# Half-size products for the keys of five more batches, with streamed weight sums and a new order inside a batch

## The chip, the core and the metric

One Trainium2 chip, one of its cores. The time is the device time of one launch, in microseconds (us). Five engines work side by side, each through its own list of instructions in order: TensorE (PE in the profile, with its weight loads as PEld), VectorE (DVE), ScalarE (ACT), GpSimd (POOL) and SyncE (SP), which issues the DMAs here. They wait for each other through semaphores.

## What is computed

Per batch (8 of them, 8 heads of width 64, 512 local and 32 global positions): windowed attention with global tokens, and behind it a feed-forward block on the joined heads (`d_model` 512, `d_ff` 1024).

```python
k_all = np.concatenate([k_g, k_l], axis=2); v_all = np.concatenate([v_g, v_l], axis=2)
out_g = sm(scale * q_g @ k_all.T) @ v_all
s_ll = np.where(np.abs(pos[:, None] - pos[None, :]) <= 32, scale * q_l @ k_l.T, -1e9)
out_l = sm(np.concatenate([scale * q_l @ k_g.T, s_ll], axis=-1)) @ np.concatenate([v_g, v_l], axis=2)
...
x_prev = x shifted by one position
xk = mu_k * x + (1.0 - mu_k) * x_prev
xr = mu_r * x + (1.0 - mu_r) * x_prev
k = np.maximum(xk @ w_k, 0.0)
v = k * k @ w_v
r = 1.0 / (1.0 + np.exp(-(xr @ w_r)))
return r * v
```

## The kernel before

The feed-forward block works on columns of 256 tokens (`TOK`), two halves per batch, and at the end on the 256 global tokens of all batches together. Each float32 operand is held as two float32r parts, a high one (`h`, a cast on ACT) and a low one (`l`, the difference, a subtraction on POOL or DVE, `split`), and a product is three matmuls: high by high, high by low, low by high. A matmul here is 128x128 weights by 128x256 tokens.

For a half batch, `mix` (L509) makes `xk` and `xr`: on DVE one difference and two scaled sums per 256 columns (L518, L522), an ACT cast (L526) and a POOL subtraction (L527). `squares` (L551) multiplies by the weights `w_k`, which stay in SBUF: 4 groups of 48 = 2x8x3 matmuls into a PSUM bank, then relu on ACT (L560) and a square on POOL (L561). `gates` (L564) takes 48 matmuls, with a copy on DVE (L577) and a sigmoid on ACT.

From batch `FROM` = 2 on, the values (the product with `w_v`) of the two halves of a batch are done together by Strassen's scheme: the 2x2 blocks of the weights (A11 to A22, and the sums S1 to S4, computed once) times the blocks of the squared keys (B11 to B22, and differences T1 to T4). Seven products of 24 matmuls stand for eight. The weight blocks lie in DRAM (`scratch`) and are loaded for each product in two parts of 512 KB into a ring of five buffers (`load_left`, L264). The token blocks are split by `Keys.split` (L635): B blocks on DVE, T blocks on POOL. `values_1` (three products) runs ahead of the keys of the first half of the next batch, `values_2` (four) ahead of those of the second, and their results are gathered by ACT copies and DVE additions (L670 to L698).

The heads of batch b+1 run beside the feed-forward of batch b: `together` advances the two streams by their share of steps. Scores land in PSUM, DVE masks them (L329), ACT takes exponentials (L335), POOL normalises (L344), PE transposes them into one bank (`ps_t`), from which ACT and DVE copy in turn (L383), and PE weights the values. The order on each engine's list is fixed when the program is built, by a list scheduler that follows the order of the code, its priorities and its own durations. SP issues all DMAs in one such list; a DMA that waits holds up those behind it. The last batch has no heads beside it, and the global tokens come last (`end`, L966).

Of the kernel before, what the change touches and what calls it, by code (L numbers as in the profile page):

```python
# [9 lines left out]
F32 = mybir.dt.float32  # L10
# [4 lines left out]
I64 = mybir.dt.int64  # L15
# [40 lines left out]
def local_global_attention_then_rwkv_ffn(  # L56
# [34 lines left out]
    ps2 = ctx.enter_context(tc.tile_pool(name="ps2", bufs=2, space=PSUM))  # L91
# [6 lines left out]
    FIRST_USE = {"m": [ps2] * 2, "s": [ps4] * 4, "t": [ps1, psx], "o": "t"}  # L98
    MIDDLE_USE = {"m": [ps2, ps2, psx], "s": [ps4] * 4, "t": [ps1], "o": "s"}
    LAST_USE = {"m": [ps2, ps2, psx, ps4, ps4, ps4, ps4]}  # L100
# [47 lines left out]
    wk_h = const.tile([P, NC, DF], F32R, name="wk_h")  # L148
    wk_l = const.tile([P, NC, DF], F32R, name="wk_l")

    early_w, early_u = ExitStack(), ExitStack()
    first_chunks = early_w.enter_context(tc.tile_pool(name="first_chunks", bufs=1, reuse_waits="tile"))
# [13 lines left out]
    def load_chunk():  # L168
        n = load_chunk.n
        if n < len(chunks):  # L170
            if n < EARLY:
                w64 = first_chunks.tile([P, CH], I64, tag=f"w64_{n}", name="w64")
            else:
                w64 = stage.tile([P, CH], I64, tag="w64", name="w64")
            nc.sync.dma_start(out=w64, in_=chunks[n][0])
            staged.append(w64)
            load_chunk.n += 1
# [41 lines left out]

    FROM = 2  # L220
    LEFT = ("A11", "A21", "A12", "A22", "S2", "S3", "S4", "S1")
    HC = NF // 2
    scratch = dramp.tile([P, len(LEFT), HC, 2, TOK], F32, name="scratch")

    def behind(store):
        tc.add_manual_dep(
            store.ins, Tokens.square.ins.name,
            mybir.DependencyInfo(mybir.DependencyClass.Sync, mybir.DependencyReason.DATA),
        )

    def sums_of_values():

        for i in range(HC):
            a = stage.tile([P, 2, 2, TOK], F32, tag="w64", name="a")
            hs, ls = (stage.tile([P, 4, TOK], F32R, tag="w64", name=f"{x}s") for x in "hl")
            for j in range(2):
                f = i + j * HC
                for x, part in enumerate((wv_h, wv_l)):
                    part = part[:, f].bitcast(F32).rearrange("p (e n) -> p e n", e=2)
                    store = nc.sync.dma_start(out=scratch[:, 2 * j:2 * j + 2, i, x], in_=part)  # L240
                    behind(store)
                with tc.issue_after(Tokens.square.ins):
                    nc.gpsimd.tensor_add(  # L243
                        a[:, j], *(w[:, f].bitcast(F32).rearrange("p (e n) -> p e n", e=2) for w in (wv_h, wv_l))
                    )
            a11, a21, a12, a22 = (a[:, j, e] for j in range(2) for e in range(2))

            nc.gpsimd.tensor_add(a22, a21, a22)
            nc.gpsimd.tensor_sub(a21, a11, a21)
            nc.gpsimd.tensor_sub(a11, a22, a11)  # L250
            nc.gpsimd.tensor_sub(a12, a12, a11)
            s = a.rearrange("p j e n -> p (j e) n")
            nc.scalar.copy(hs, s)
            nc.vector.tensor_sub(ls, s, hs.bitcast(F32))
            for x, part in enumerate((hs, ls)):
                nc.sync.dma_start(out=scratch[:, 4:8, i, x], in_=part.bitcast(F32))
            yield

    V1 = (("A11", "B11"), ("A12", "B21"), ("S2", "T2"))
    V2 = (("S3", "T3"), ("S1", "T1"), ("A22", "T4"), ("S4", "B22"))  # L260
    to_load = [a for a, _ in V1 + V2] * (B - FROM) + ["A11", "A21", "A12", "A22"]
    left = []

    def load_left():  # L264
        if to_load:
            a = LEFT.index(to_load.pop(0))
            for i in range(0, HC, 2):
                part = leftp.tile([P, 2, 2, TOK], F32R, tag="a", name="a")
                nc.sync.dma_start(out=part.bitcast(F32), in_=scratch[:, a, i:i + 2])
                left.append(part)  # L270
# [226 lines left out]
    class Tokens:  # L497
# [5 lines left out]
        def two(self, pool, name, dtype=F32, tag="tmp"):  # L503
            return pool.tile([P, 2, TOK], dtype, tag=tag, name=name)
# [4 lines left out]
        def mix(self):  # L509

            got = []
            for mu, nm in ((mu_k_sb, "k"), (mu_r_sb, "r")):
                got.append((mu, self.wide(f"x{nm}h", F32R), self.wide(f"x{nm}l", F32R)))
            for c0 in range(0, NC, 2):
# [4 lines left out]
                for mu, hi, lo in got:  # L519
                    xf = self.two(tmpp, "xfull")  # L520
                    for j in range(2):
# [3 lines left out]
                        )  # L525
                    nc.scalar.copy(hi[:, both], xf)  # L526
# [74 lines left out]

    class Keys:


        def __init__(self, tokens):
            self.tokens = tokens
            self.k, self.parts = {}, {}

# [5 lines left out]
        def block(self, name):  # L614
            if name in ("B12", "B22"):
                tag = {"B12": "kkh0", "B22": "kkh2"}[name]
                self.k[name] = [self.tokens[0].two(mlp, name, tag=tag) for _ in range(2)]
# [5 lines left out]
        def keys(self, t):  # L623
# [11 lines left out]
        def split(self, *names):  # L635
            for b in names:
                self.parts[b] = []
                for val in self.k[b]:
                    tags = Keys.PARTS[Keys.n_parts % len(Keys.PARTS)]
                    Keys.n_parts += 1  # L640
                    h, l = (self.tokens[0].two(mlp, f"b{x}", F32R, tag) for x, tag in zip("hl", tags))
# [3 lines left out]
        def product(self, out, b, fresh=True):  # L645
            right = self.parts.pop(b)
            for i in range(HC):
                a, (b_h, b_l) = left[i // 2], right[i // 2]
                for j in range(2):
                    a_h, a_l = (a[:, i % 2, x, j * P:(j + 1) * P] for x in range(2))  # L650
                    for n, (w, x) in enumerate(((a_h, b_h), (a_h, b_l), (a_l, b_h))):
                        nc.tensor.matmul(  # L652
                            out[:, j], w, x[:, i % 2], start=fresh and (i, j, n) == (0, 0, 0),
                            stop=(i, n) == (HC - 1, 2), skip_group_check=True,
                        )
            del left[:HC // 2]
            load_left()

        def bank(self):
            return psum("m").rearrange("p (j n) -> p j n", j=2)  # L660

        def sum(self):
            return sump.tile([P, 2, TOK], F32, tag="sum", name="sum")

        def values_1(self):
            t = self.tokens[0]
            X, Y = self.bank(), self.bank()
            self.product(X, "B11")
            c11, self.u2 = self.sum(), self.sum()
            nc.scalar.copy(c11, X)  # L670
            yield
            self.product(Y, "B21")
            nc.vector.tensor_add(c11, Y, c11)
            t.write(0, c11)
            yield
            self.product(X, "T2", fresh=False)
            nc.scalar.copy(self.u2, X)
            yield
            self.split("T3", "T1", "T4")

        def values_2(self):
            t0, t1 = self.tokens
            u2, u3 = self.u2, self.sum()
            X, Y = self.bank(), self.bank()
            self.product(X, "T3")
            nc.vector.tensor_add(X, X, u2)
            nc.scalar.copy(u3, X)
            self.split("B22")
            yield
            self.product(Y, "T1")  # L690
# [345 lines left out]
```

## Time and profile before

| | us |
|---|---|
| three runs: median (lowest, highest) | 715.65 (714.83, 717.27) |
| the profiled execution, whole | 714.27 |
| its span, first to last instruction | 712.1 |
| PE busy in the span | 670.7 |
| DVE, ACT, POOL busy | 413.5, 421.4, 412.8 |

A busy PE in this profile is not PE at its peak: matmuls overlap, and each lasts about 280 ns in the rows although the next starts much sooner. So PE's cost is read from starts, not from busy time. DVE and POOL rows can hold waiting too: an instruction that was issued and could not go on counts as busy. A stage of a batch with heads beside it shows twice, as two halves of some 38 us.

### The profile page before, as it was taken

What the parts mean: (1) busy time and instruction counts of PE and PEld (TensorE: products, weight loads), DVE (VectorE), ACT (ScalarE), POOL (GpSimd) and SP (SyncE); (2) the same over time, 40 slices, a digit from 0 to 9 for tenths busy, and PEclk for the clock granted to TensorE, in tenths of its full rate; (3) what the DMA queues carried; (4) which work ended last, traced back from release to release, by engine and by line L of the source; (5) the groups of instructions that cost most, each with busy time, mean ns of one, the idle gap of its engine ahead of it and who ended that gap; (6) DMA issues with size and microseconds to landing.
All of it is one profiled execution on the core that took longest, in us unless ns stands there. A gap on an engine that the chain in (4) does not pass through costs nothing.

```text
span 712.1 us, 18675 instructions
## 1 busy us (share of the span) xinstructions
PE 670.7 (94%) x7472; PEld 627.4 (88%) x7472; DVE 413.5 (58%) x1180; ACT 421.4 (59%) x1135; POOL 412.8 (58%) x415
## 2 busy tenths in 40 slices
PE   5779899999899899889999999999999999999997
PEld 3568788889798899789999999999989999999896
DVE  5757886346647563756566365735674556276441
ACT  5857787547556557664848384767567553442530
POOL 6556595236858555565567655585558444854730
PEclk9669999999999999999999999999999999999999
DMA  8731635052756652270928265554827090535666
GB/s 344 278 118 37 246 97 216 31 187 83 234 175 201 220 194 75 85 271 8 356 83 282 76 257 188 170 186 143 304 92 265 2 332 24 192 119 164 197 195 200
DMA packets 43542, 123.37 MB, mean 173 GB/s; under 512 B 4032, under 2 KB 20928, under 8 KB 43456
## 3 DMA queue, kind: packets, MB, share of 16 engines
q1 hardware_dynamic: 43456, 122.18, 49.1%
q8 instruction: 59, 0.97, 0.6%
q14 instruction: 27, 0.22, 0.1%
HBM read 104.86 MB, written 17.30 MB: 172 GB/s over the span
## 4 chain that ended last, share of the span: by engine, by line
PE 46%; ACT 16%; DVE 14%; POOL 10%; issue 7%; DMA 6%; POOLq 0%; SPq 0%; ACTq 0%; DVEq 0%
PE ps_m L652 13%; PE ps_m L495 7%; PE ps_m L493 7%; PE ps_m L494 7%; PE ps_s L360 7%; ACT Pt L335 6%; DVE xfull L522 5%; POOL B L561 2%; DVE diff L518 2%; PE ps_t L381 2%; DMA a<-scratch 2%; POOL Pt L344 1%; DMA w<-w_r 1%; DVE B L633 1%; POOL a L243 1%
## 5 line engine op out<-in xcount | busy, mean ns | idle before, releaser
L493 PE MATMUL ps_m<-xkh,wk_h 128*128 128x256 f32 x544 | 154.4, 285 | 5.3 <-ACT gate L573 1.9
L495 PE MATMUL ps_m<-xkh,wk_l 128*128 128x256 f32 x544 | 152.7, 281 | 0.0
L494 PE MATMUL ps_m<-xkl,wk_h 128*128 128x256 f32 x544 | 152.2, 280 | 0.4 <-POOL xkl L527 0.4
L652 PE MATMUL ps_m<-bh,a 128*128 128x256 f32 x736 | 136.3, 281 | 1.5 <-DMA a<-scratch 0.9
L335 ACT ACTIVATE Pt<-Pt,m 128x160 f32<-128x160 f32 x256 | 106.4, 418 | 21.5 <-DVE m L329 21.4
L652 PEld LDWEIGHTS ps_m<-bh,a 128*128 128x128 f32 x736 | 114.3, 188 | 3.7 <-issue 1.5
L344 POOL TENSOR_TENSOR Pt<-Pt,ssum 128x512 f32<-128x512 f32 x64 | 68.2, 1065 | 82.7 <-DVE ssum L293 80.0
L493 PEld LDWEIGHTS ps_m<-xkh,wk_h 128*128 128x128 f32 x544 | 102.9, 190 | 7.8 <-ACT gate L573 2.3
L494 PEld LDWEIGHTS ps_m<-xkl,wk_h 128*128 128x128 f32 x544 | 103.0, 189 | 0.7 <-POOL xkl L527 0.7
L495 PEld LDWEIGHTS ps_m<-xkh,wk_l 128*128 128x128 f32 x544 | 103.1, 189 | 0.0
L652 PE MATMUL ps_m<-bl,a 128*128 128x256 f32 x368 | 102.8, 279 | 0.0
L561 POOL TENSOR_TENSOR B<-relu 128x512 f32<-128x512 f32 x52 | 56.3, 1089 | 39.1 <-ACT relu L560 39.0
L493 PE MATMUL ps_m<-xrh,wr_h 128*128 128x256 f32 x272 | 78.3, 288 | 0.0
L495 PE MATMUL ps_m<-xrh,wr_l 128*128 128x256 f32 x272 | 77.8, 287 | 0.0
L494 PE MATMUL ps_m<-xrl,wr_h 128*128 128x256 f32 x272 | 77.3, 284 | 0.0
L527 POOL TENSOR_TENSOR xkl<-xfull,xkh 128x512 fp32r<-128x512 f32 x34 | 45.3, 1333 | 54.1 <-ACT xkh L526 38.1
L560 ACT ACTIVATE relu<-ps_m 128x512 f32<-128x512 f32 x52 | 31.0, 596 | 76.7 <-PE ps_m L495 73.9
L329 DVE CUSTOM_DVE_ANT_0 Pt<-ps_s,masks 128x160 f32<-128x160 f32 x256 | 65.5, 317 | 8.9 <-PE ps_s L360 8.7
L652 PEld LDWEIGHTS ps_m<-bl,a 128*128 128x128 f32 x368 | 69.1, 188 | 0.6 <-issue 0.6
L518 DVE TENSOR_TENSOR diff<-xT 128x256 f32<-128x256 f32 x64 | 41.9, 693 | 33.7 <-ACT xT L485 19.9
L203 ACT CAST bh<-B 128x512 fp32r<-128x512 f32 x76 | 45.4, 625 | 16.2 <-PE ps_m L652 13.7
L495 PEld LDWEIGHTS ps_m<-xrh,wr_l 128*128 128x128 f32 x272 | 51.8, 191 | 3.0 <-issue 2.8
(144 smaller groups left out, 1639.2 us busy)
## 6 DMA issues: line engine op xcount, KB each, us to landing
a<-scratch SPq DMA_DIRECT2D x92, 512.0 KB, 6.0
raw_qk<-qk SPq DMA_DIRECT2D x32, 768.0 KB, 5.7
raw_v<-v SPq DMA_DIRECT2D x32, 640.0 KB, 5.9
out_l<-gate SPq DMA_DIRECT2D x32, 256.0 KB, 4.9
w<-w_k SPq DMA_DIRECT2D x8, 512.0 KB, 9.8
w<-w_v SPq DMA_DIRECT2D x8, 512.0 KB, 5.2
w<-w_r SPq DMA_DIRECT2D x4, 512.0 KB, 4.9
scratch<-wv_h SPq DMA_DIRECT2D x8, 256.0 KB, 2.9
```

Of the source, the lines that this page charges most:

```text
L203: nc.scalar.copy(hi, val)
L329: read = nc.vector.tensor_tensor_reduce(out=Pt[:, i], in0=place(e, t, h), in1=masks[:, e, slots[t][1]], op0=ALU.add, op1=ALU.min, scale=-s ...
L335: nc.scalar.activation(Pt[:, i], Pt[:, i], AF.Exp, bias=low_x[:, i:i + 1], scale=-1.0, accum_out=ssum[:, i:i + 1],)
L344: nc.gpsimd.tensor_mul(out, Pt[:, each, at:at + n], rinv.unsqueeze(2).to_broadcast([P, 4, n]))
L360: self.last = nc.tensor.matmul(*a, **kw)
L493: nc.tensor.matmul(out, w_h[:, i, cols], x_h(i), start=(i == 0), stop=False)
L494: nc.tensor.matmul(out, w_h[:, i, cols], x_l(i), start=False, stop=False)
L495: nc.tensor.matmul(out, w_l[:, i, cols], x_h(i), start=False, stop=(i == n - 1))
L518: nc.vector.tensor_sub(self.shape(diff[:, j]), self.cur(c0 + j), self.prev(c0 + j))
L527: nc.gpsimd.tensor_sub(lo[:, both], xf, hi[:, both].bitcast(F32))
L561: nc.gpsimd.tensor_mul(k2[f0 // HC][f0 % HC // 2], rk, rk)
L652: nc.tensor.matmul(out[:, j], w, x[:, i % 2], start=fresh and (i, j, n) == (0, 0, 0), stop=(i, n) == (HC - 1, 2), skip_group_check=True,)
```

## The change

From batch 3 on (`FROM` + 1) the keys too are done by seven products instead of eight. The weight blocks of `w_k` and their sums are made during batch 2 (`sums_of_keys`) into a second DRAM tensor, and `w_k` leaves SBUF after that. All weight blocks, 14 parts for the values and 14 for the keys of a batch, come through one ring of six buffers of 512 KB. The token side of the keys is mixed as four blocks for the whole batch, subtracted on DVE and split on ACT and POOL (`mixed`, `x_split`). Both kinds of product go through `seven`, on three PSUM banks. A batch now goes: values of the batch before, gate of half 0, keys, gate of half 1. The last keys of the global tokens are plain products with loaded blocks.

```diff
-    FIRST_USE = {"m": [ps2] * 2, "s": [ps4] * 4, "t": [ps1, psx], "o": "t"}
-    MIDDLE_USE = {"m": [ps2, ps2, psx], "s": [ps4] * 4, "t": [ps1], "o": "s"}
+    FIRST_USE = {"m": [psa, psb], "s": [ps4] * 4, "t": [ps1, psx], "o": "t"}
+    MIDDLE_USE = {"m": [psa, psb, psx], "s": [ps4] * 4, "t": [ps1], "o": "s"}
...
+    def sums(home, tag, parts, out, first, after):
+        a = home.tile([P, 2, 2, TOK], F32, tag=tag, name="a")
...
+            add = first.tensor_add(a[:, j], parts(0, j), parts(1, j))
...
+        nc.gpsimd.tensor_add(a22, a21, a22)
+        nc.gpsimd.tensor_sub(a21, a11, a21)
+        nc.gpsimd.tensor_sub(a11, a22, a11)
+        nc.gpsimd.tensor_sub(a12, a12, a11)
...
+    for b in range(FROM, B - 1):
+        plan(of_values, [a for a, _ in SEVEN])
+        plan(of_keys, [a for a, _ in SEVEN], True)
...
+    def product(out, right, fresh=True):
+        for i, (b_h, b_l) in enumerate(right):
+            a, home = left.pop(0)
...
+            load_left(home)
+            yield
+    def seven(right, done):
+        X, Y, Z = new_bank(), new_bank(), new_bank()
...
+        yield from product(X, right("B11"))
+        copy(c11, X)
+        yield from product(Y, right("B21"))
+        add(Y, c11, 0, 0)
+        yield from product(X, right("T2"), fresh=False)
+        copy(u2, X)
+        yield from product(Z, right("T1"))
+        copy(w, Z)
+        yield from product(X, right("T3"), fresh=False)
+        add(X, w, 1, 1)
+        yield from product(Z, right("B22"), fresh=False)
+        add(Z, u2, 0, 1)
+        yield from product(X, right("T4"), fresh=False)
+        done(1, 0, X)
...
+        def mixed(self):
+            B11, B21, B12, B22 = (self.xv[f"B{i}{j}"] for j in (1, 2) for i in (1, 2))
+            self.x_split("B11", B11)
+            self.x_split("B21", B21)
+            nc.vector.tensor_sub(B11, B12, B11)
+            nc.vector.tensor_sub(B12, B22, B12)
+            self.x_split("B22", B22)
+            nc.vector.tensor_sub(B22, B22, B11)
+            self.x_split("T2", B22)
+            self.x_split("T1", B11)
+            nc.vector.tensor_sub(B21, B21, B22)
+            self.x_split("T3", B12)
+            self.x_split("T4", B21)
+        def x_split(self, name, val):
+            self.x[name] = h, l = [Tokens.two(kxp, f"x{name}{x}", F32R, name + x) for x in "hl"]
+            split(val, h, l, nc.gpsimd)
...
+                def done(i, j, v):
+                    if in_psum(v):
...
+                    else:
+                        nc.vector.scalar_tensor_tensor(blocks[i, j][n], v, 0.0, v, op0=ALU.max, op1=ALU.mult)
...
-        for n, t in enumerate(this.tokens):
-            t.mix()
-            if b > FROM:
-                yield from (before.values_1, before.values_2)[n]()
...
-            yield from this.keys(t)
...
+        this.mix(0)
+        for n, _ in enumerate(before.values()):
+            yield
+            if n == 4:
+                this.mix(1)
+            if n == 8:
+                this.mixed()
+        yield from this.tokens[0].gates()
...
+        yield from this.keys()
+        this.split("B11", "B21")
+        this.differences()
+        this.split("T2")
+        yield from this.tokens[1].gates()
```

How the lists of the engines change. The first place is POOL's list where the keys of a batch end and the values of it begin. Before (batch 5; `B` is a block of squared keys, `xkl` and `xrl` low parts of the mixed tokens, `bl` low part of a value operand, `Pt` the attention weights):

```order
L561 TENSOR_TENSOR B_7321<-relu 128x512
L204 TENSOR_TENSOR bl<-T_7528,bh 128x512
L561 TENSOR_TENSOR B_7322<-relu 128x512
L527 TENSOR_TENSOR xkl<-xfull,xkh 128x512
L344 TENSOR_TENSOR Pt<-Pt,ssum 128x4x128
L344 TENSOR_TENSOR Pgl<-Pt,ssum 128x128
L344 TENSOR_TENSOR Pt<-Pt,ssum 128x4x128
L344 TENSOR_TENSOR Pgl<-Pt,ssum 128x128
L527 TENSOR_TENSOR xrl<-xfull,xrh 128x512
L418 TENSOR_SCALAR Pg<-Pg,ssumg 128x576
```

The same place in the change, from the square of the last product of the keys on (`xB11l`, `xT1l` and the like are low parts of the keys' token blocks):

```order
L742 TENSOR_TENSOR B_7280<-relu 128x512
L205 TENSOR_TENSOR xB11l<-xB_7843,xB11h 128x512
L571 TENSOR_TENSOR xrl<-xfull,xrh 128x512
L205 TENSOR_TENSOR xB21l<-xB_7844,xB21h 128x512
L571 TENSOR_TENSOR xrl<-xfull,xrh 128x512
L205 TENSOR_TENSOR bl<-T_7759,bh 128x512
L571 TENSOR_TENSOR xrl<-xfull,xrh 128x512
L205 TENSOR_TENSOR bl<-B_7279,bh 128x512
L205 TENSOR_TENSOR xT1l<-xB_7843,xT1h 128x512
L205 TENSOR_TENSOR bl<-B_7279,bh 128x512
L205 TENSOR_TENSOR xB22l<-xB_8039,xB22h 128x512
L205 TENSOR_TENSOR bl<-B_7281,bh 128x512
```

The splits of the whole next batch now stand between those of the values, up to T4's (`bl<-B_7280`, eleven rows further on); before, a half batch's mix stood here and the other half's came half a batch later.

The second place is DVE's list at the same time, behind the last addition of the keys, up to a part of what stands ahead of the next copy of transposed weights (`PT<-ps_t`):

```order
L744 SCALAR_TENSOR_TENSOR B_7282<-u_7471 128x512
L771 TENSOR_TENSOR B_7279<-B_7282,B_7279 128x512
L560 TENSOR_TENSOR diff<-xT 128x256 x2
L771 TENSOR_TENSOR T_7759<-B_7284,B_7279 128x512
L771 TENSOR_TENSOR B_7282<-B_7284,B_7282 128x512
L564 SCALAR_TENSOR_TENSOR xB_7843<-diff,mu_k_sb,xT 128x256
L564 SCALAR_TENSOR_TENSOR xfull<-diff,mu_r_sb,xT 128x256
L564 SCALAR_TENSOR_TENSOR xB_7843<-diff,mu_k_sb,xT 128x256
L564 SCALAR_TENSOR_TENSOR xfull<-diff,mu_r_sb,xT 128x256
L205 TENSOR_TENSOR bl<-B_7280,bh 128x512
L518 COPY xg_all<-ps_s 128x2x32
```

Both halves' mixes, 24 instructions, now follow here in one run; before, each half's twelve stood apart.

The third place is PE's list in batch 5 of the change, with the semaphores it waits for, early in the values' last product (T4). The L531 to L533 rows are matmuls of the gate, L469 transposes the global attention weights:

```order
L532 MATMUL ps_m<-xrl,wr_h 128x256
L533 MATMUL ps_m<-xrh,wr_l 128x256
L531 MATMUL ps_m<-xrh,wr_h 128x256
L469 MATMUL ps_t<-ident,Pg 128x128 [waits Activation_49]
L469 MATMUL ps_t<-ident,Pg 128x128 x3
L654 MATMUL ps_m<-bl,a 128x256 [waits Pool_49]
L654 MATMUL ps_m<-bh,a 128x256 x2
```

The product's first matmul stands ahead of ten matmuls of the gate, of which three are shown; its second one waits for POOL's split of T4. Before, keys stood between a split on POOL and the product that used it.

334 lines of the change are left out of this document (185 added, 149 removed).

## The prediction

> **What bounds the kernel now.** I read the page's totals first, then a table by stage, then single rows of the timeline. The page:
>
> ```profile
> span 712.1 us, 18675 instructions
> PE 670.7 (94%) x7472; PEld 627.4 (88%) x7472; DVE 413.5 (58%) x1180; ACT 421.4 (59%) x1135; POOL 412.8 (58%) x415
> L493 PE MATMUL ps_m<-xkh,wk_h 128*128 128x256 f32 x544 | 154.4, 285 | 5.3 <-ACT gate L573 1.9
> a<-scratch SPq DMA_DIRECT2D x92, 512.0 KB, 6.0
> ```
>
> PE is busy almost all the time and nothing else is near it. The table by stage (columns: length, then busy time of PE, PEld, DVE, ACT, POOL with counts, granted clock, DMA share, GB/s) says where it isn't:
>
> ```profile
> 240.00:280.00 40.00, 40.00 (x469) 38.23 (x468) 20.65 (x77) 27.65 (x83) 16.93 (x18) 1.00 0.43 151
> 280.00:318.40 38.40, 33.38 (x405) 30.91 (x404) 24.11 (x69) 23.50 (x65) 26.65 (x25) 1.00 0.46 163
> 438.00:476.30 38.30, 38.05 (x452) 36.05 (x451) 22.07 (x70) 24.89 (x69) 26.44 (x26) 1.00 0.50 166
> 476.30:514.50 38.20, 38.15 (x454) 36.63 (x453) 22.20 (x70) 24.36 (x68) 20.37 (x21) 1.00 0.58 208
> 650.00:665.00 15.00, 13.74 (x117) 13.36 (x115) 14.16 (x20) 4.02 (x7) 8.27 (x6) 1.00 0.32 95
> ```
>
> In the steady batches (third and fourth row, the halves of one) PE idles 0.3 us in 76.5. It idles 5.0 us where the values first go by half-size products (second row) and 1.3 us early in the end stage (last row). So PE bounds the steady batches, and matmuls taken away are worth their spacing. The chain that ended last gives that spacing:
>
> ```profile
> 636.64 5.44 PE ps_m L652 x48
> 601.43 4.02 PE ps_s L360 x117
> ```
>
> 48 matmuls in 5.44 us are 0.1133 us each, and not the 285 ns that one lasts. The 456 matmuls of a batch take 51.7 us; the rest of the 76.5, 24.8 us, is two pairs of heads, 12.4 each. The second row is the largest piece of a pair, the weighting.
>
> **Matmuls taken away.** The keys of a half batch are 96 matmuls (L493 to L495: 544 of each is 17 halves of 32). A batch's 192 become two times seven products of 12, 168. Five batches (3 to 7) save 120, and 120 x 0.1133 is **-13.6 us**. The products of global keys keep their 96.
>
> **The port that DVE and POOL share.** The work around the matmuls decides what is left of this. Here is a place of before where DVE, POOL and PE meet:
>
> ```profile
> 284.99 1.51 DVE L633 TENSOR_TENSOR B<-B,B 128x512 f32<-128x512 f32 x1 [3.64 <-POOL B L561]
> 286.43 1.52 DVE L633 TENSOR_TENSOR T<-B,B 128x512 f32<-128x512 f32 x1
> 288.48 0.68 DVE L383 COPY PT<-ps_t 128x512 f32<-128x512 f32 x1
> ...
> 283.92 3.48 POOL L561 TENSOR_TENSOR B<-relu 128x512 f32<-128x512 f32 x3
> ...
> 289.21 0.44 PE L390 MATMUL ps_t<-ident,Pgl 128*128 128x128 f32 x2 [1.93 <-DVE PT L383]
> ```
>
> While POOL's three squares run (283.92 to 287.40), two DVE subtractions take 1.5 us each; the copy behind them is late, and PE waits 1.93 us for it. Alone, such work starts faster. DVE first, then POOL:
>
> ```profile
> 650.84 0.69 DVE L633 TENSOR_TENSOR T<-B,B 128x512 f32<-128x512 f32 x1 [2.09 <-POOL B L561]
> 651.45 0.69 DVE L633 TENSOR_TENSOR B<-B,B 128x512 f32<-128x512 f32 x1
> ...
> 458.23 0.76 DVE L518 TENSOR_TENSOR diff<-xT 128x256 f32<-128x256 f32 x2 [2.54 <-ACT xT L485]
> 458.91 0.48 DVE L522 SCALAR_TENSOR_TENSOR xfull<-diff,mu_k_sb,xT 128x256 f32<-128x256 f32 x1
> 459.31 0.48 DVE L522 SCALAR_TENSOR_TENSOR xfull<-diff,mu_r_sb,xT 128x256 f32<-128x256 f32 x1
> ...
> 667.24 1.30 POOL L527 TENSOR_TENSOR xkl<-xfull,xkh 128x512 fp32r<-128x512 f32 x1
> 668.49 1.29 POOL L527 TENSOR_TENSOR xrl<-xfull,xrh 128x512 fp32r<-128x512 f32 x1
> ...
> 676.02 2.04 POOL L561 TENSOR_TENSOR B<-relu 128x512 f32<-128x512 f32 x2
> ...
> 298.55 0.40 POOL L344 TENSOR_TENSOR Pgl<-Pt,ssum 128x128 f32<-128x128 f32 x1
> 298.90 1.04 POOL L344 TENSOR_TENSOR Pt<-Pt,ssum 128x512 f32<-128x512 f32 x1
> ...
> 303.85 0.74 POOL L418 TENSOR_SCALAR Pg<-Pg,ssumg 128x576 f32<-128x576 f32 x1 [1.04 <-DVE ssumg L293]
> ```
>
> From start to start: a 512-column DVE operation with both operands in SBUF 0.60, a difference 0.34, a scaled sum 0.40; a POOL split 1.25, a square 1.02, `Pt` with `Pgl` 1.35, `Pg` 0.74. A DVE operation that reads PSUM runs beside POOL's at its normal time:
>
> ```profile
> 463.98 0.68 DVE L383 COPY PT<-ps_t 128x512 f32<-128x512 f32 x1
> ...
> 464.00 1.27 POOL L204 TENSOR_TENSOR bl<-B,bh 128x512 fp32r<-128x512 f32 x1
> ```
>
> So I count POOL's work and DVE's two-SBUF work as one queue. How exact that is: three squares alone are 3.06 us and took 3.48 with one DVE subtraction slipped between, so that 0.60 cost 0.42.
>
> **What the new order puts into one stretch.** Take a steady batch of the change (4, 5, 6), from the last matmul of the keys to the second half of the values' last product, T4, which waits for POOL. Before its split POOL's list holds 7 splits of key blocks, 4 of `xr`, 7 of value parts and a gate product (19 x 1.25 = 23.8), a square (1.0), two `Pt` pairs (2.7) and one `Pg` (0.7): 28.2 us. DVE's list holds, up to the addition which the same product waits for, 8 differences (2.7), 16 scaled sums (6.4) and 12 operations of 512 columns (7.2): 16.3. The queue is **44.5 us**. It starts about 0.9 us before the last keys' matmul, at the addition behind the sixth product. PE has 196 matmuls there (22.2) and one pair of heads (12.4): 34.6. The wait is 44.5 - 0.9 - 34.6 = **9.0 us** a batch if nothing overlaps. With DVE's part at 0.42 for 0.60 it is 11.4 instead of 16.3, and the wait 4.1. Neither row is nearer, and I take the middle, 6.5. Queued behind the waiting matmul are the rest of the gate, the weighting of heads and the next keys, all of PE's work, so nothing covers it. Before, the same work was spread over both halves, with a mix of 12 DVE operations each, and fitted.
>
> [...]
>
> Batch 3 has less on POOL (23.0) and 16.4 on DVE against 198 matmuls (22.4) and most of a pair (11.6): 0 to 4.5 us, middle 2.3. In batch 7, without heads, POOL has 24.6 and DVE 19.0 against 257 matmuls (29.1) and one weighting (4.0): 3.9 to 9.6, middle 6.8. New waits: 2.3 + 3 x 6.5 + 6.8 = **28.6 us** (16.2 to 41.1).
>
> **Waits that go.** The 5.0 and 1.3 us of the table by stage lie in stretches counted anew: **-6.3 us**.
>
> **The rest.** The sums of the keys' weights in batch 2 add 16 small POOL operations, 8 additions of 512 columns and 4 of 1024 on DVE, some 23 us of the queue, in a stage (240 to 280) where PE never idles and POOL is busy 16.9 of 40. If all of DVE's 20.65 there were two-SBUF work, 60.6 would have to fit in 40, 20.6 over; with half of it, 10 over, of which the batch's later half takes some. I take 0, since its results are due only in batch 3, and keep 6 for the range. ACT has 19 operations of some 0.6 us more in five batches, and with 24.9 busy of 38.3 room for them beside PE. Between two products on bank X stands one of 12 matmuls (1.36 us), in which ACT must copy 512 columns:
>
> ```profile
> L670 ACT COPY sum<-ps_m x6: 562/578/586, 303.5 to 664.8; 128x512 f32<-128x512 f32 x6
> ```
>
> Its 0.58 us fit, with 0.8 to spare; 0 is taken, and what it costs if ACT is late is a rival. SP issues 78 more loads of weight parts and 24 stores.
>
> Sum, against the profiled execution's 714.27 (712.1 span and 2.2 around it; the median of the runs is 1.4 higher): -13.6 + 28.6 - 6.3 = +8.7, **723 us**. By the ends of the waits, -3.7 to +21.2: 710.6 to 735.5.
>
> **The rivals.**
> *The queue doesn't reach PE* (other side). Gate matmuls hoisted into gaps and DVE work done earlier could hide it: the place is the same stretch, and it decides where the waits sum to less than the 19.9 us that the matmuls and the waits gone are worth, four a batch. For it: in before, the steady halves hold POOL 26.4 and DVE 22.1 in 38.3, and PE doesn't idle. Against it: the lists, in which T4's split comes behind all key splits. With 6 us left of the new waits: 714.3 - 19.9 + 6 = 700.
>
> *Loads bound PE.* 170 parts instead of 92, 14 per kind of product with one every 1.36 us, and a part lands 6.0 us after issue. Six buffers give five parts ahead, 6.8 us. Before, with five, PE waited in its last run of products:
>
> ```profile
> 702.72 0.35 PE L652 MATMUL ps_m<-bh,a 128*128 128x256 f32 x1 [0.45 <-DMA a<-scratch]
> 300.00:310.00 10.00, 8.58 (x157) 8.18 (x157) 2.32 (x9) 7.25 (x17) 6.42 (x7) 1.00 0.85 319
> ```
>
> At 319 GB/s for a share of 0.85, a pair of `qk` loads (1.5 MB) holds the queues 4.2 us, which leaves 3.4 us of wait after 0.8 of margin. Half of the sixteen pairs of loads in batches 3 to 6 falling on products cost 27: 714.3 - 13.6 + 27 = 728, if the shared port costs nothing. Against it: heads between the products stretch the lead.
>
> *Three banks turn too slowly.* If ACT's copy comes 1.1 us late, 0.3 over the margin, at four turns of each of ten key products of seven, that is 12 us, and the gain is gone: 713.
>
> **How the numbers follow.** Queue 0.58 (723, 711 to 736), hidden queue 0.25 (700), loads 0.09 (728), banks 0.08 (713). About 0.3%, 2.1 us, is what a measurement of this kernel can tell from no change. Of the first case I give 0.50 to slower, 0.05 to same, 0.03 to faster, as its low end lies below no change; with the loads 0.09 to slower and 0.01 of the banks: slower 0.60. Faster is 0.25 and 0.03, 0.28; same 0.12. The range goes from 700, which cuts half of the hidden queue, to 738, the upper end with part of batch 2's 6 us. The likeliest case's own range is 711 to 736.
>
> **What would show it.** Right: PE idles for POOL's `bl` or a DVE copy or addition around the values' last products, 4 to 9 us in each of batches 4 to 7; DVE's differences and scaled sums there last over 1 us. Wrong: steady batches of about 73.8 us with PE idle under 1 us (the first rival); idle time ended by DMA `a` (the second), or by ACT copies of `u2` and `w` in the keys (the third). The saving is right if the steady batch, less its waits, is 2.7 us shorter than 76.5.

## The result and the profile after

The changed kernel takes **760.29 us** (median of 4 runs, 759.36 to 763.87) and the kernel before, on the same chip, 715.63 (4 runs, 714.83 to 717.27): 1.063 times the time, 95% interval 1.0591 to 1.0669. It is slower, as forecast, but by 45 us and not by 9. The profiled executions differ as much: 759.94 against 714.27.

The page of the changed kernel, its totals, two of its groups (busy us, mean ns of one, idle time before and what ended it) and its loads of weight parts (KB each, us from issue to landing):

```profile
span 757.8 us, 18783 instructions
PE 679.9 (90%) x7352; PEld 632.1 (83%) x7352; DVE 517.3 (68%) x1266; ACT 434.3 (57%) x1154; POOL 439.9 (58%) x416
L560 DVE TENSOR_TENSOR diff<-xT 128x256 f32<-128x256 f32 x64 | 52.6, 859 | 9.3 <-ACT xT L523 9.2
L564 DVE SCALAR_TENSOR_TENSOR xfull<-diff,mu_r_sb,xT 128x256 f32<-128x256 f32 x64 | 49.8, 798 | 2.1 <-POOL xkl L571 2.1
a<-scratch_v SPq DMA_DIRECT2D x92, 512.0 KB, 5.2
a<-scratch_k SPq DMA_DIRECT2D x78, 512.0 KB, 4.7
```

PE does 120 matmuls fewer and is busy 9 us longer; DVE is busy 104 us longer with only 86 instructions more. The loads land sooner, in 5.2 and 4.7 us against the 6.0 of before, although there are 78 more.

The table by stage (length, then busy time of PE, PEld, DVE, ACT, POOL with counts, granted clock, DMA share, GB/s). First the kernel before, from 240 us to its end:

```profile
240.00:712.10 472.10, 459.06 (x5107) 441.32 (x5105) 259.26 (x705) 265.21 (x689) 265.61 (x247) 1.00 0.50 171
```

Then the changed kernel: the same stage, its parts between the ends of pairs of heads (batch 2's keys and gates with the first of batch 3's values, then batches 3 to 6 with their overlaps, then batch 7 and the end), and last a stretch of the values and one of the keys:

```profile
240.00:757.80 517.80, 466.95 (x4999) 444.58 (x4997) 362.54 (x796) 274.65 (x706) 292.62 (x250) 0.96 0.73 249
231.50:322.30 90.80, 80.23 (x896) 74.67 (x894) 63.09 (x151) 53.24 (x140) 64.55 (x63) 0.96 0.69 239
322.30:399.60 77.30, 71.67 (x827) 66.24 (x820) 57.50 (x153) 46.92 (x136) 41.65 (x38) 0.98 0.75 251
399.60:477.90 78.30, 72.49 (x842) 68.46 (x841) 58.54 (x152) 47.29 (x137) 45.42 (x40) 0.96 0.80 267
477.90:564.50 86.60, 77.45 (x884) 73.30 (x882) 63.54 (x155) 50.93 (x142) 49.06 (x43) 0.94 0.77 256
564.50:646.70 82.20, 71.62 (x794) 68.64 (x793) 58.55 (x112) 41.62 (x101) 42.50 (x35) 0.96 0.72 233
646.70:757.80 111.10, 99.26 (x844) 98.65 (x843) 67.76 (x87) 37.67 (x64) 56.03 (x40) 0.97 0.71 255
...
480.00:500.00 20.00, 11.53 (x98) 10.76 (x98) 20.00 (x41) 11.66 (x21) 14.32 (x11) 0.77 0.39 115
520.00:540.00 20.00, 20.00 (x276) 19.32 (x275) 8.69 (x30) 11.82 (x32) 0.06 (x1) 1.00 0.90 301
```

All of the 45.7 us lie after 240 us (517.8 - 472.1). PE's idle time there went from 472.1 - 459.1 = 13.0 to 517.8 - 467.0 = 50.9, **+37.8**. Its busy time rose by 7.9 although the stage holds 108 matmuls fewer (5107 - 4999, 12.2 us; at 240 us the changed kernel is 12 matmuls behind, 1.4 us). So **20.1** us of busy time are new as well. The last two rows show where: at 480 to 500, in the values, where the lists of DVE and POOL are both full (the crowded stretch, or the crowd, from here on), DVE is busy without a break and PE for 11.5 of 20; at 520 to 540, in the keys, PE is full, DVE half idle and POOL has nothing to do.

The waits of PE in the changed kernel after 240 us (us in total, times, longest):

```profile
PE ps_t L428 <- DVE PT L421: 24.0, 7, 6.7
PE ps_m L654 <- ACT u L679: 8.0, 1, 8.0
PE ps_t L419 <- ACT PT L421: 7.7, 4, 3.1
PE ps_s L400 <- DVE xT L520: 2.6, 1, 2.6
...
PE ps_m L654 <- DMA a<-scratch_k: 0.9, 1, 0.9
```

The largest is the turn of the one bank of the transposes: `Pgl` can't be transposed into it until DVE has copied `PT` out. One such wait in the timeline, PE, then DVE and POOL:

```profile
407.48 0.28 PE L654 MATMUL ps_m<-bl,a 128*128 128x256 f32 x1
413.29 0.69 PE L428 MATMUL ps_t<-ident,Pgl 128*128 128x128 f32 x2 [5.54 <-DVE PT L421]
...
414.42 0.63 PE L654 MATMUL ps_m<-bh,a 128*128 128x256 f32 x2
414.85 0.41 PE L654 MATMUL ps_m<-bl,a 128*128 128x256 f32 x1
415.06 0.63 PE L654 MATMUL ps_m<-bh,a 128*128 128x256 f32 x2
...
405.79 2.36 DVE L564 SCALAR_TENSOR_TENSOR xfull<-diff,mu_r_sb,xT 128x256 f32<-128x256 f32 x2
408.07 1.75 DVE L720 TENSOR_TENSOR xB<-xB,xB 128x512 f32<-128x512 f32 x1
409.75 2.89 DVE L560 TENSOR_TENSOR diff<-xT 128x256 f32<-128x256 f32 x2
412.56 0.68 DVE L421 COPY PT<-ps_t 128x512 f32<-128x512 f32 x1
...
407.83 1.45 POOL L571 TENSOR_TENSOR xrl<-xfull,xrh 128x512 fp32r<-128x512 f32 x1
409.24 1.72 POOL L643 TENSOR_TENSOR gate<-c,gate 128x512 f32<-128x512 f32 x1
410.91 1.44 POOL L571 TENSOR_TENSOR xrl<-xfull,xrh 128x512 fp32r<-128x512 f32 x1
```

Two things are to be read here. The `PT` copy itself takes 0.68 as ever (all 32 of them on DVE last 676 to 693 ns), but stands behind five DVE operations with both operands in SBUF, 2.1 us of work at their times alone (two of 0.40, one of 0.60, two of 0.34) by the prediction's rows. Here they take 6.8 us, about as long each as one of POOL's operations beside them, which last 1.44 to 1.72. And when PE goes on, three matmuls take 0.64 us (414.42 to 415.06), 0.213 each instead of 0.1133: **half clock**. The granted clock over this and the next such stretch:

```profile
412.00:419.00 7.00, 5.71 (x46) 5.37 (x50) 5.98 (x24) 5.79 (x22) 3.22 (x4) 0.51 0.74 192
490.00:501.00 11.00, 6.02 (x29) 6.03 (x30) 10.96 (x27) 5.67 (x16) 8.99 (x7) 0.53 0.23 73
```

There are seven stretches of half clock after 240 us (from 275, 302, 343, 412, 490, 579 and 664 on), 3.4 to 10.2 us long, one at each of the seven waits of 2.55 us or more that end there: five of them set in before the wait's end, those from 275 and 343 on 0.3 and 1.0 us after it. Before had none there: its clock is 1.00 in the first row of the stage table. The seven are 40.8 us long together, and PE is busy for 29.6 of them at a granted clock of 0.50, so they cost about 15 us of the 20.1. The other 5 are slightly wider spacing elsewhere, which I can't assign. The length of a wait alone doesn't decide: a wait of 2.72 us that ends at 239.4 us in the same profile, and one of 2.03 at 236 us in the kernel before, were followed by a clock of 1.00.

Three of the seven stretches (from 275, 302 and 343 on) are 3.4 us long, three (from 412, 579 and 664 on) 6.8 and the one from 490 on 10.2. The shortest wait that one came with is 2.55 us here, and 1.8 in run e10.

The wait of 8.0 us in batch 7 comes by way of ACT, whose copy `u` frees a bank of the products:

```profile
663.76 2.88 DVE L564 SCALAR_TENSOR_TENSOR xfull<-diff,mu_r_sb,xT 128x256 f32<-128x256 f32 x2
...
666.68 0.62 ACT L570 CAST xrh<-xfull 128x512 fp32r<-128x512 f32 x1 [2.19 <-DVE xfull L564]
667.20 0.58 ACT L679 COPY u<-ps_m 128x512 f32<-128x512 f32 x1
```

The copy stands behind a cast that waits for DVE's late `xfull`.

### The profile page after: what moved, and what is told of

The parts are those of the page before. It is cut to its first block, busy times and chain, and to the rows that moved or that the text cites. A ratio compares the mean times of both kernels' runs of the same rounds, so it can differ in the third digit from the quotient of the medians.

```text
span 757.8 us, 18783 instructions
## 1 busy us (share of the span) xinstructions
PE 679.9 (90%) x7352; PEld 632.1 (83%) x7352; DVE 517.3 (68%) x1266; ACT 434.3 (57%) x1154; POOL 439.9 (58%) x416
## 4 chain that ended last, share of the span: by engine, by line
PE 46%; DVE 26%; ACT 14%; POOL 6%; issue 5%; DMA 3%; SPq 0%; DVEq 0%; ACTq 0%; POOLq 0%
PE ps_m L654 20%; DVE xfull L564 5%; PE ps_s L398 5%; PE ps_m L531 5%; ACT Pt L373 5%; PE ps_m L532 5%; PE ps_m L533 5%; DVE diff L560 5%; DVE xB L564 3%; DVE B L771 3%; PE ps_t L419 2%; DVE Pt L367 2%; PE ps_t L394 1%; POOL a L244 1%; DVE PT L421 1%
## 5 line engine op out<-in xcount | busy, mean ns | idle before, releaser
L654 PEld LDWEIGHTS ps_m<-bh,a 128*128 128x128 f32 x736 | 119.7, 197 | 12.2 <-ACT u L679 8.2
L531 PE MATMUL ps_m<-xrh,wr_h 128*128 128x256 f32 x272 | 79.5, 292 | 0.0
L533 PE MATMUL ps_m<-xrh,wr_l 128*128 128x256 f32 x272 | 79.1, 292 | 0.0
L531 PE MATMUL ps_m<-xkh,wk_h 128*128 128x256 f32 x192 | 57.9, 304 | 1.9 <-ACT xkh L570 1.5
L560 DVE TENSOR_TENSOR diff<-xT 128x256 f32<-128x256 f32 x64 | 52.6, 859 | 9.3 <-ACT xT L523 9.2
L532 PE MATMUL ps_m<-xkl,wk_h 128*128 128x256 f32 x192 | 57.4, 300 | 1.1 <-POOL xkl L571 1.0
L533 PE MATMUL ps_m<-xkh,wk_l 128*128 128x256 f32 x192 | 56.1, 293 | 0.0
L531 PEld LDWEIGHTS ps_m<-xrh,wr_h 128*128 128x128 f32 x272 | 53.7, 197 | 1.3 <-ACT Pt L373 0.6
L533 PEld LDWEIGHTS ps_m<-xrh,wr_l 128*128 128x128 f32 x272 | 53.7, 198 | 0.8 <-issue 0.6
L532 PEld LDWEIGHTS ps_m<-xrl,wr_h 128*128 128x128 f32 x272 | 53.7, 197 | 0.6 <-issue 0.2
L571 POOL TENSOR_TENSOR xrl<-xfull,xrh 128x512 fp32r<-128x512 f32 x34 | 49.8, 1465 | 5.4 <-ACT xrh L570 5.3
L419 PE MATMUL ps_t<-ident,Pt 128*128 128x128 f32 x256 | 41.1, 287 | 13.0 <-ACT PT L421 10.4
L205 POOL TENSOR_TENSOR bl<-B,bh 128x512 fp32r<-128x512 f32 x36 | 49.6, 1385 | 4.4 <-ACT bh L204 4.4
L564 DVE SCALAR_TENSOR_TENSOR xfull<-diff,mu_r_sb,xT 128x256 f32<-128x256 f32 x64 | 49.8, 798 | 2.1 <-POOL xkl L571 2.1
```

The costliest lines, as they stand in the source:

```text
L205: engine.tensor_sub(lo, val, hi.bitcast(F32))
L419: nc.tensor.transpose(tp[:, i], r.Pt[:, 4 * e + i, SG * e:SG * e + W], ident)
L531: nc.tensor.matmul(out, w_h[:, i, cols], x_h(i), start=(i == 0), stop=False)
L532: nc.tensor.matmul(out, w_h[:, i, cols], x_l(i), start=False, stop=False)
L533: nc.tensor.matmul(out, w_l[:, i, cols], x_h(i), start=False, stop=(i == n - 1))
L560: nc.vector.tensor_sub(self.shape(diff[:, j]), self.cur(c0 + j), self.prev(c0 + j))
```

## The experiments

Times are medians of four runs, with those of the kernel before on the same chip between 714.4 and 716.5. They are set against the changed kernel's 760.29.

**e1 and e2: POOL's low parts of the key blocks**, moved to DVE, and left out.

```diff
-            split(val, h, l, nc.gpsimd)
+            split(val, h, l, nc.vector)      # e1
+            nc.scalar.copy(h, val)           # e2
+            self.x[name] = h, h
```

> Changed kernel, with the low parts of the seven key blocks of a batch (L731, 35 in all) subtracted on DVE and not on POOL. In the changed kernel's profile DVE's differences and scaled sums take 0.40 us alone and 1.45 to 1.50 where POOL has a split in hand (1.44 each), and PE waits 24 us for DVE's PT copies behind them. Theory A, the two engines take turns at SBUF: each of the 35 costs the shared queue 0.60 instead of 1.25, 23 us less in the five stretches, and DVE's small operations are no longer held up one by one; about half of the 42 us of waits in batches 3 to 7 and of the 16 us at half clock go: 725 to 738 us. Rival B, DVE simply has too much work of its own: it gets 35 x 0.60 = 21 us more, the copies come later: 775 to 785. Rival C, only the place of the PT copy in the order matters: 755 to 765.

> Changed kernel without the 35 low parts of the key blocks: the high part is used in their place, so that part of the computation is left out, with the same matmuls, loads and DVE work. Theory A (DVE and POOL take turns at SBUF): 35 x 1.25 = 44 us less in the shared queue of batches 3 to 7, the waits there (42 us) nearly go, and with them some 14 us of half clock: 700 to 715 us. Rival B (DVE has too much work of its own) and rival C (only the place of the PT copy): DVE's list is the same, 750 to 765.

e1: 758.07 us (755.93 to 760.09), no change that can be told. e2: 748.49, 11.8 less. Rival C fits e1 and fails in e2; theory A has the sign of e2 and a quarter of its size. Moving 35 operations to DVE, where one takes 0.60 us alone against POOL's 1.25, gave nothing.

**e3: all `PT` copies on ACT.**

```diff
-        copy = nc.vector.tensor_copy if e else nc.scalar.copy
+        copy = nc.scalar.copy
```

> Changed kernel with all PT copies on ACT (the second of each pair was on DVE). Rival C, the one bank of the transposes and the place of its DVE copy in the order is the cause: the 24 us that PE waits for DVE's PT and some 10 us of half clock behind them go: 722 to 732 us. Theory A, the shared queue is the cause and the copy only the first place at which it reaches PE: DVE's and POOL's lists are no shorter, the next thing due from them (DVE's additions, POOL's splits of the last products, the splits of the key blocks) is late instead: 738 to 755.

759.68 us. Rival C falls, and theory A's range is missed as well, by 5 us. PE's waits in e3:

```profile
PE ps_t L419 <- ACT PTg L429: 12.4, 4, 6.0
PE ps_m L654 <- ACT u L679: 7.5, 2, 5.8
PE ps_t L428 <- ACT PT L421: 7.1, 3, 4.6
PE ps_s L400 <- DVE m L367: 4.8, 1, 4.8
```

The wait for DVE's `PT` is gone and others have come, on ACT's copies and on DVE's reduction of the scores: the bank was only the first place at which a late engine reached PE.

**e4: the sums of the keys' weights without their arithmetic.**

```diff
-                sums(
...
+                        for lo in (2 * j, 4 + 2 * j):
+                            behind(Tokens.square, nc.sync.dma_start(out=scratch_k[:, lo:lo + 2, s, i, x], in_=part))
```

> Changed kernel without the arithmetic of the sums of the keys' weights in batch 2: the unsummed blocks are stored in their place (same transfers; left out are 8 + 4 operations on DVE, 16 on POOL, 4 on ACT). If these sums cost what PE waits in the later half of batch 2 (2.7 + 0.4 + 0.8 + 4.2 us at 272 to 303 of the changed kernel, and two stretches of half clock, about 2 us): 748 to 752 us. If those waits come from the mix of batch 3 and the values' differences alone, as I forecast when I gave the sums 0: 757 to 763.

753.08 us (752.65 to 754.83), 7.2 less: the sums that I gave nothing cost about 7 us.

**e5: 12 differences of a batch left out on DVE.** The edit takes the `tensor_sub` lines out of `differences()` and of `mixed()`.

> Changed kernel without 12 differences of a batch on DVE (the 8 of differences(), the 4 of mixed(); the blocks themselves are used in their place, so that part of the computation is left out): 60 operations, 36 us at 0.60 each, with POOL, PE, ACT and the loads unchanged. The run without POOL's splits of the key blocks took away 44 us of POOL and gave 11.5. Theory A (POOL's and DVE's work is one queue, an us of either is worth the same): 36 us are worth 9 to 10, 748 to 753. Theory D (DVE's own list is what PE waits for; POOL only stretches its operations to 1.45): 60 operations off the list are worth nearly all waits of batches 3 to 7 and their half clock: 715 to 730.

741.09 us, 19.2 less. The pages count DVE's operations as 1198 against 1266, so 68 are left out and not 60: `differences()` runs in batch 2 too. These 68 operations, 41 us alone, give 1.6 times what 44 us of POOL gave. It lies between the theories. An operation of DVE is worth about 0.28 us (the 0.32 of later expectations counts 60).

**e6: all of POOL's low parts of batches 3 to 7 left out.**

```diff
-                    nc.gpsimd.tensor_sub(lo[:, both], xf, hi[:, both].bitcast(F32))
+                    if lo is not hi:
+                        nc.gpsimd.tensor_sub(lo[:, both], xf, hi[:, both].bitcast(F32))
...
-            split(val, h, l, nc.gpsimd)
+            h = Tokens.two(kxp, f"x{name}h", F32R, name + "h")
+            nc.scalar.copy(h, val)
+            self.x[name] = h, h
...
+                    if b[0] == "T":
...
+                        nc.scalar.copy(h, val)
+                        self.parts[b].append((h, h))
```

> Changed kernel without any low part that POOL subtracts in batches 3 to 7 for key blocks, gate and the values' differences (the high part stands in): 19 operations a batch, 119 us of POOL in all are left out, DVE's list is unchanged. DVE then runs nearly at its times alone. If the shared port alone makes DVE late: no waits of over 2 us behind DVE's PT copies in batches 4 to 7, 702 to 715 us. Theory D, DVE's list is too long for its place even alone: waits of 2 to 4 us a batch stay there, 728 to 742.

720.77 us, 39.5 less, between the two expectations. The pages count POOL's operations as 313 against 416, so 103 are left out: 19 in each of five batches and the 8 for batch 2's differences, 129 us at 1.25 each and not 119. DVE's list is the same, and its groups and PE's waits for it are now:

```profile
L567 DVE SCALAR_TENSOR_TENSOR xfull<-diff,mu_r_sb,xT 128x256 f32<-128x256 f32 x64 | 38.3, 616 | 2.1 <-POOL xkl L575 2.1
L563 DVE TENSOR_TENSOR diff<-xT 128x256 f32<-128x256 f32 x64 | 35.3, 588 | 12.0 <-ACT xT L523 11.9
PE ps_t L428 <- DVE PT L421: 2.8, 3, 1.9
```

A difference takes 588 ns instead of 859 and the waits for `PT` fall from 24.0 to 2.8. So the most part is what POOL's work does to DVE's times: none of PE's own waits after 240 us in the changed kernel ends with POOL. That 720.77 isn't lower goes with batch 2, whose sums this edit leaves alone (a wait of 2.5 us at 272 us and two stretches of half clock), and with a wait of 2 to 3 us in each of batches 5 and 6.

**e7: the gate's second mix held back to the keys.** `mix_gate()`, with its own differences, is tied to a product of the keys.

> Changed kernel with the gate's mix of the second half batch held back to the keys (batches 3 to 6), where POOL and DVE have idle time: four scaled sums and two POOL splits a batch leave the crowded stretch, four differences are added in the keys. Theory D: 4 operations of up to 1.45 us fewer ahead of the late copies, 4 to 5 us a batch with the half clock: 740 to 748. Theory A: 4 x 0.40 + 2 x 1.25 = 4.1 us of 44 in the queue, some 1 us a batch by the run without the key blocks' splits: 755 to 758.

772.18 us, 12 more. The edit did not do what it meant: the tie was to an instruction of PE and didn't hold DVE, which ran the repeated differences in the crowd, ahead of `PT`:

```profile
409.69 2.89 DVE L556 TENSOR_TENSOR diff<-xT 128x256 f32<-128x256 f32 x2
```

So it tells of something else: 16 differences more on DVE, 5.4 us alone, and the changed order around them cost 12.

**e8: the second half's mix behind the `PT` copy in DVE's order.**

```diff
-                this.mix(1)
+                with tc.issue_after(transposes.last.ins):
+                    this.mix(1)
```

> Changed kernel with the mix of the second half batch (4 differences, 8 scaled sums) ordered behind DVE's PT copy, which stood behind most of it; nothing is left out. Rival C (the place of the copies in DVE's order is the cause): the waits for DVE's PT in batches 3 to 7 (some 19 us) and about 8 us of half clock behind them go: 732 to 740 us. Theories A and D (the list itself is too long): the key blocks come later and PE waits for them or for DVE's additions instead: 750 to 763.

760.20 us, no change. PE's waits for DVE's `PT` fall from 24.0 to 6.6, and others take their place:

```profile
PE ps_t L419 <- ACT PT L421: 9.7, 5, 3.9
PE ps_m L656 <- ACT u L681: 9.1, 3, 8.0
PE ps_s L400 <- DVE m L367: 8.0, 3, 5.0
```

**e9: part of the mix done ahead, in the keys of the batch before** (`mix_ahead()` after the eighth of the keys' steps; `mix_rest()` does what is left).

> Changed kernel with part of the mix of batches 4 to 7 done ahead, in the keys of the batch before, where DVE is half idle and POOL wholly (first pair of channel chunks: 4 differences, 6 scaled sums on DVE, 1 split on POOL a batch); 2 differences a batch are computed twice for it, nothing is left out. If the crowd in one stretch is what costs (theories A and D): net 8 DVE operations fewer there in four batches, 32, at 0.32 us each (19 us for 60 in the run without differences) 10 us, and at the 0.75 that 16 added ones cost 24: 736 to 750. If the sum of the work on the port over the batch counts, wherever it stands: 758 to 764.

757.82 us (757.27 to 759.19), 2.5 less, at the edge of the second expectation, and the theory of the crowd missed: the waits for DVE's `PT` sink to 13.9, but PE now waits in the keys too (377, 460 and 466 us into the span, 2 us each). The crowd is not one stretch alone.

**e10: e4, e5 and e6 together.**

> Three edits that were run singly together: without POOL's low parts of batches 3 to 7 (gave 39.5 us), without the 60 differences on DVE (19.2), without the arithmetic of the sums in batch 2 (7.2); all that is left out of the computation, matmuls and loads are whole. Theory: only the crowded port, DVE's list in it and the half clock behind the waits eat the saved matmuls; with them gone what is left is the time before less 120 matmuls (13.6 us) and less some of the waits of before: 696 to 703 us, no row of half clock after 310 us. If loads of the weight parts or turns of the three banks cost too: over 708, with PE waiting for DMA or for ACT's copies.

705.19 us, 0.9877 of the time before (0.985 to 0.9905), two us over my bound. Its stage from 240 us and its waits:

```profile
240.00:705.70 465.70, 454.13 (x5002) 435.19 (x5002) 237.88 (x717) 269.69 (x702) 121.64 (x131) 0.99 0.80 277
PE ps_t L418 <- ACT PT L420: 4.1, 3, 2.6
...
PE ps_m L657 <- ACT u L682: 1.8, 1, 1.8
...
PE ps_m L657 <- DMA a<-scratch_k: 1.0, 1, 1.0
```

The loads run at 277 GB/s and cost PE 1.0 us, the turns of the products' banks 1.8. Two stretches of half clock of 3.4 us are left (the mean clock of the stage is 0.99), from 240 us behind a wait of 2.6 and from 397 behind the wait of 1.8 for `u`; the second is one that the expectation ruled out. With POOL's low parts, the differences of DVE's list and most of the half clock out of the way the saved matmuls are there: 9.7 us by the medians, with PE's idle time at 11.6 us (465.7 - 454.1) about that of before.

**e11 and e14: POOL's subtractions put back into e6 with results that nobody reads.** In e11 each reads the high part twice, in e14 the value and its high part, as in the changed kernel.

```diff
+            nc.gpsimd.tensor_sub(Tokens.two(kxp, "junk", tag="junk"), h.bitcast(F32), h.bitcast(F32))    # e11
+            nc.gpsimd.tensor_sub(Tokens.two(kxp, "junk", tag="junk"), val, h.bitcast(F32))    # e14
```

> The run without POOL's low parts (720.8 us), with as many POOL subtractions of the same size put back (19 a batch but 2), whose results go to a spare tile and are read by nobody; PE still uses the high parts in place of the low ones, so the low parts are left out of the computation. If it is the shared port that POOL's work costs: the time goes back up, 748 to 765 us, DVE's scaled sums last 0.8 on average as in the changed kernel. If it was the waiting for POOL's results (DVE's buffers, PE's operands): it stays at 719 to 728.

> As e11 (POOL's subtractions put back, results to a spare tile), but each reads the same two tiles as in the changed kernel, the value and its high part, so that DVE must wait for POOL before it writes a buffer anew. The low parts stay left out for PE. If the other half of POOL's cost is that DVE waits for its buffers: 752 to 762 us. If it is PE's wait for the low parts themselves: 735 to 743, as e11.

e11: 739.61 us, half of the 39.5 back, between the two expectations. e14: 756.29 (753.61 to 759.07), nearly all of it back. The subtractions themselves, e11 and then e14:

```profile
L791 POOL TENSOR_TENSOR junk<-bh 128x512 f32<-128x512 f32 x46 | 53.0, 1151 | 49.2 <-ACT bh L789 47.7 <-DMA a<-scratch_v 0.2
...
L791 POOL TENSOR_TENSOR junk<-B,bh 128x512 f32<-128x512 f32 x36 | 48.7, 1353 | 25.1 <-ACT bh L789 23.5
L567 DVE SCALAR_TENSOR_TENSOR xfull<-diff,mu_r_sb,xT 128x256 f32<-128x256 f32 x64 | 44.7, 717 | 10.5 <-POOL junk L577 8.4 <-POOL xkl L575 2.1
```

Nobody reads these results, so PE's wait for the low parts is not what they cost; that POOL works on SBUF at that time costs most of the half that e11 shows: DVE's scaled sums for the gate (`xfull`) last 734 ns there, 616 in e6 and 798 in the changed kernel. One wait of PE in e11, 2.6 us, is ended by a POOL subtraction itself and doesn't go by way of DVE. Between e11 and e14 two things differ, and I can't part them: a subtraction of two tiles is longer (1353 against 1151 ns), and DVE now waits for tiles that POOL still reads (8.4 us in the last row; the changed kernel itself has next to none of this). So e14 comes back to nearly the same time by partly another path: PE waits 7.5 us for DVE's `PT` there and not 24.0, and 10.8 and 10.0 for ACT's `u` and `PTg`.

**e12 and e13: work moved to ACT with nothing left out**: the normalising of `Pt`, and then sums kept in PSUM and squares on ACT too.

```diff
+                for i in range(4 * e, 4 * e + 4):
+                    part = Pt[:, i, SG * e:SG * e + W]
+                    nc.scalar.activation(part, part, AF.Copy, scale=ssum[:, i:i + 1])    # e12, e13
...
+            out = bank if stay and bank is not X else sum    # e13
...
-                nc.vector.tensor_add(sum, bank, sum)
+                nc.vector.tensor_add(out, bank, sum)    # e13
...
-                        nc.vector.scalar_tensor_tensor(blocks[i, j][n], v, 0.0, v, op0=ALU.max, op1=ALU.mult)
+                        nc.scalar.activation(v, v, AF.Relu)    # e13
+                        nc.scalar.activation(blocks[i, j][n], v, AF.Square)    # e13
```

> Changed kernel with the normalising of Pt (8 operations of 1.0 us a batch on POOL, for the heads of batches 3 to 7) on ACT instead, 32 operations of 128 columns a batch; nothing is left out. Theory (each us of work on the port costs; 119 us of POOL left out gave 39.5, 44 gave 11.8, so 0.27 to 0.33 an us): 40 us of POOL in five batches give 11 to 13 us: 746 to 750. Rival (no gain without taking DVE's work or the waits for POOL's low parts away, as when work was moved between DVE and POOL): 756 to 763, or more if ACT is late.

> As e12, and the sums of the values' second and fifth results stay in PSUM, so that their gate products go from POOL to DVE with one PSUM operand (2 x 1.25 us of POOL a batch), and the six squares of a batch's keys' sums go from DVE to ACT (6 x 0.60 us of two-SBUF work); nothing is left out. Theory: 52 us of POOL at 0.3 and 30 DVE operations at 0.32 each: 760 - 16 - 10 = 734, 728 to 740. Rival (moved work gives nothing): 754 to 763. Only under 714 would it beat both kernels.

780.33 us, 20 more, and 765.14, 5 more. The theory missed by 30 both times. In e12 POOL is busy 388.9 us instead of 439.9 and DVE 483.5 instead of 517.3, and PE waits for ACT:

```profile
PE ps_t L474 <- ACT PG L475: 15.1, 5, 4.0
PE ps_m L659 <- ACT c L684: 9.9, 4, 3.9
```

ACT's copies out of PSUM, 0.58 us each, now stand behind 32 more operations a batch. No version with the whole computation came near the kernel before.

## Why the prediction was right in sign and wrong in size

- *Matmuls taken away, -13.6.* Nothing speaks against it: e10 shows 9.7 by the medians, with two stretches of half clock left.
- *The shared port, new waits of 28.6.* "Port" in the prediction and the expectations is my name for what the rows show of DVE and POOL on SBUF; no run shows a port itself. That POOL's work on SBUF holds up DVE is shown by e6 and e11 (a scaled sum 616 ns without POOL's low parts, 734 with its subtractions back; and, by partly another path, e14); the place was wrong, and the size too low. I let DVE and POOL's work run through as one queue and looked for its end, at the split of T4, where PE then never waited. But in the crowd one operation of DVE goes with one of POOL: DVE's scaled sums and differences, 0.34 to 0.40 alone, take 1.45 beside POOL's 1.44 (485.2 to 494.3 us), so DVE's list falls behind early, and the first of DVE's copies that PE needs is `PT`, in the middle of the values. In batch 7 it is ACT that stands behind DVE's list and copies `u2` late, and PE waits 8.0 us where I took 6.8. Batches 3 to 6 idle 5.6, 5.8, 9.2 and 10.6 us (the rows from 322.30 to 646.70 of the stage table, length less PE), where I took 2.3 for batch 3 and 6.5 for each of the others, with 4.5 and 9.0 as bounds. That batches 4 to 7 come near my numbers is in part luck, since the waits stand at another place than the one that I counted up to.
- *The wait of 9.0 if nothing overlaps.* In the rows above a DVE operation lasts as long as POOL's 1.44. The 9.0 a batch was the nearer one in batches 5 and 6 (9.2 and 10.6), my 6.5 in batch 4 (5.8).
- *Waits that go, -6.3.* Wrong: the first part of the stage table idles 10.6 us (90.8 - 80.2), 2.7 of them ahead of 240 us. The 7.9 that are left stand against 5.0 of before from 240 to 318 us, the stretch that I quoted.
- *Batch 2's sums, 0.* Wrong: e4 measures 7.2, waits and half clock together, a little over the 6 that I kept for the range only.
- *Loads and banks cost nothing.* Right: 1 us waited for DMA, and a part lands in 5.2 and 4.7 us where it took 6.0; the rivals of loads and banks fall as causes of their own.

Net, the waits were to bring 28.6 - 6.3 = 22.3 and brought 37.8, 15.5 more. The larger part of the miss of 37 us (45.7 - 8.7) is **a term that the sum did not have**: I priced a wait at its own length, and PE's busy time came out 20.1 us above what the matmuls taken away leave of it. About 15 of these are half clock at seven of the waits. With 37.8 for the waits the sum would still have ended at 738.5 (714.3 - 13.6 + 37.8), at the top of the range. The profile of before could have told it. Between 20 and 60 us, where PE waits a lot, its clock (third number from the end) is 0.66 and 0.74, and it is 1.00 in all the stages that I quoted:

```profile
20.00:40.00 20.00, 15.70 (x153) 11.75 (x153) 16.56 (x55) 13.95 (x41) 12.29 (x14) 0.66 0.67 254
40.00:60.00 20.00, 15.75 (x146) 12.47 (x143) 11.90 (x43) 12.64 (x43) 9.25 (x10) 0.74 0.17 55
```

What stays open: how e14's last 17 us part into DVE's longer operations and its waits for buffers, the 5 us of wider spacing, and what besides its length decides whether half clock comes with a wait.

## What to carry to other kernels

Price a wait of PE at more than its length: half clock came with seven waits of 2.55 to 8.0 us here and cost about 2 us a wait (15 us in all), though none came with one of 2.72; look in the profile's clock row for what the kernel's own waits have cost. Where DVE and POOL both work on SBUF, count operations and not only their time: in the crowd here each of DVE's with both operands in SBUF took as long as one of POOL's (1.45 beside 1.44, 0.34 to 0.40 alone), and PE waited up to 6.7 us for what it needed next of DVE, the `PT` copy. And if taking work away makes a kernel faster, but moving the same work between engines or in the order does not (no change in e1, e3 and e8, -2.5 us in e9, +20 in e12, +5 in e13), the engines around PE are full, and a change that trades matmuls for their work must be weighed against that.

## What the runs showed of the hardware that was not expected

- DVE's scaled sum of 256 columns took 0.40 us alone and 1.45 to 1.5 beside POOL's subtractions of 1.44. From 485.2 to 494.3 us of the changed kernel six operations of DVE and six of POOL alternate so, one for one.
- Half clock came with waits of 2.55 us (changed kernel) and of 1.8 (e10), and not with waits of 2.72 (changed kernel, at 236.7 us) and of 2.03 (kernel before). In e10 the wait at 237 us, 2.6 us long, was followed by half clock, and the one at the same place in the changed kernel was not.
- POOL's subtraction of 512 columns took 1.15 us on the mean where both operands were the same tile (e11; one at 571.0 us took 1.04) and 1.35 where they were two tiles (e14).
